# Folding two half-masked key blocks into one square per head in a windowed attention ahead of two FFNs

## Chip, cores, metric

One core of one Trainium2 chip. The metric is the device time of one execution in microseconds (us), the median of several. Work runs on TensorE (PE; its weight loads are listed as PEld), VectorE (DVE), ScalarE (ACT), GpSimd (POOL), and on DMA transfers that SyncE (SP) issues.

## The reference

Three stages in fp32, on a batch of 4, 8 heads, 576 positions and 64 values per head (2304 tokens of 512 values). The attention is causal with a window of 128 keys and a linear bias per head:

```python
rel = pos[:, None] - pos[None, :]
mask = (rel >= 0) & (rel < 128)
scores = where(mask, q @ k.T / 8 - slope[h] * abs(rel), -1e9)
attn = softmax(scores);  x = attn @ v                       # tokens x 512
h = x @ w_in;  u = h * softmax(h)                            # w_in 512 x 1024
x = ((u - mean(u)) / sqrt(var(u) + 1e-6) * g_ln) @ w_out     # w_out 1024 x 512
out = (silu(x @ w_gate) * (x @ w_val)) @ w_out2              # width 1536
```

A tile of 128 queries needs two key blocks of 128: its own block, where the keys j <= i (indices inside the block) count, and the block before, where the keys j > i count. The two masks are complements of each other. The first query tile of a batch element has only its own block.

## The kernel before

The attention runs over 20 query tiles (4 batch elements, 5 tiles t = 0 to 4; the last of each has 64 queries) and over 4 pairs of heads in each: 80 units. `score` (L329) multiplies queries by the two key blocks of two units in fp32 into one PSUM bank per unit: per head 256 columns, the block before at 0 and the own block at 128. `attend` (L368) then does, for one unit:

- L390, DVE, once per head: scores plus bias from PSUM to the tile `e` in SBUF, with the row extreme (the profile calls it CUSTOM_DVE_ANT_0, with a small accumulator read behind it);
- L395, ACT, once per head: exponential with the row sum, which is put into the same PSUM bank;
- L400 and L401, DVE: the inverse of the sums; L406 (ACT) or L408 (POOL, DVE): `e` times the inverse, both heads;
- L429, PE: each 128x128 block of `e` is turned against `ident` into a second PSUM bank, 4 turns per unit (2 where t is 0);
- L433 to L438, ACT or DVE: that bank is copied into `pt` in SBUF;
- L461, PE: values times probabilities, both blocks of keys accumulated for each head.

When the last unit of a query tile is through, its output goes to `xs` as a high and a low fp32r part (`high` L211, `low` L215), and the first FFN takes tiles of 128 tokens: `up` (L547), `flip` (L609), `down1` (L638). All its products, and those of the second FFN, are emitted by `pieces` (L539, matmuls at L543). The weights are 64-bit and are decoded on ACT, DVE and POOL (`decode`, L223): 8 blocks of `w_in` and 8 of `w_out` while the attention starts, 36 of the second FFN's later. `second_region` (L686) gives the attention's SBUF to the second FFN once the last unit is done, and starts its decoding and `gate_val` and `down` from there.

`slope` (L314) makes the scaled bias tables; `load` (L292) issues the loads of queries, keys and values through SP, and in its first call those of `base` and `ident`.

The order on every engine is made when the program is built: `Emitter` (L79) keeps the operations that could run, costs them with the formulas at L193 to L203, and gives each engine the next by earliest start and then by rank. The engines follow that order strictly; DVE operations marked `+` and POOL operations are planned as excluding each other. Eight PSUM banks (`bank_s`) are shared by all steps of this stretch; `e` has 5 buffers (EB), `pt` 3 (PTB), `v` 3, `xs` 3.

Of the kernel before, what the change touches and what calls it, by code (L numbers as in the profile page):

```python
# [17 lines left out]
B, H, S, D = 4, 8, 576, 64  # L18
NT = B * S
DM = H * D  # L20
DF1 = 1024
DF2 = 1536
P = 128
# [15 lines left out]
PXB = 2  # L39
EB = 5  # L40
PTB = 3
YS = 2
PW_2 = -0.5
LEAD = 3.2
# [136 lines left out]


@with_exitstack
def attention_then_two_ffns(ctx: ExitStack, tc: tile.TileContext, qk, v, w_in, w_out, g_ln, w2, ident_d, base_d, out):
# [22 lines left out]
    ident = const.tile([P, P], F32, name="ident")  # L207
# [82 lines left out]
    ident_ok = []  # L290

    def load(c):  # L292

        b, t = steps[c]
        n = P if t < 4 else 64
        yield raw_s
        raw[c] = [at.tile([P, 4, P], F32, tag=f"raw{x}", bufs=RAW, name=f"raw{x}") for x in range(2)]
        got = [[], []]
        for j in range(2) if c == 0 else (0,):
            part = slice(2 * j, 2 * j + 2) if c == 0 else slice(0, 4)  # L300
            for x in range(2):
                got[j].append((yield dma(raw[c][x][:, part], qk[b, t, x, :, part], 131072 if c == 0 else 262144)))
            if c == 0 and j == 0:
                chain((yield dma(base, base_d, 196608)), base_ok)
                ident_ok.append((yield dma(ident, ident_d, 65536)))
        yield v_s
        vt[c] = at.tile([P, DM], F32, tag="v", bufs=3, name="v")
        loaded[c] = yield dma(vt[c][0:n], v[b, t * P:t * P + n, :], 262144)
        for j in range(2):
            for x in got[j]:  # L310
                yield x
            prepped[c][j].settle(x.time)

    def slope(part, h):  # L314

        cs = slice(2 * P, 3 * P) if part == 0 else slice(0, 2 * P)
        n = P if part == 0 else 2 * P
# [50 lines left out]
    def attend(u):  # L368
        c, pr = divmod(u, NPAIR)
        b, t = steps[c]  # L370
        n = P if t < 4 else 64
        if t == 0:
            bs, cols, order = slice(2 * P, 3 * P), P, [1]
        elif t < 4:
            bs, cols, order = slice(P, 3 * P), 2 * P, [0, 1]
        else:
            bs, cols, order = slice(P, 2 * P + 64), P + 64, [0, 1]
        yield scored[c][pr]
        k, x = begun[u]
        sc = banks[k]  # L380
        e = at.tile([P, 2, 256], F32, tag="e", bufs=EB, name="e")
        st = at.tile([P, 8], F32, tag="st", bufs=EB, name="st")
        d = x
        for j in range(2):
            yield bias_ok[0][2 * pr + j]
            if t:
                yield bias_ok[1][2 * pr + j]
        ex, ds = [], []
        for j in range(2):
            d = yield (DVE, t_dve(cols), lambda j=j: nc.vector.tensor_tensor_reduce(  # L390
                e[0:n, j, 0:cols], sc[0:n, j * 256:j * 256 + cols], bias[0:n, 2 * pr + j, bs],
                -0.125, 3.0e38, ALU.add, ALU.min, st[0:n, j:j + 1]), [x])
            ds.append(d)
        for j, d in enumerate(ds):
            ex.append((yield (ACT, 93 + t_act(cols, True, True), lambda j=j: nc.scalar.activation(  # L395
                e[0:n, j, 0:cols], e[0:n, j, 0:cols], AF.Exp, bias=st[0:n, j:j + 1], scale=-1.0,
                accum_out=sc[0:n, j:j + 1]), [d, ds[0]])))

        def invert():
# [3 lines left out]
        def normalize(eng):  # L403
            if eng is nc.scalar:
                for j in range(2):
                    nc.scalar.activation(e[0:n, j, 0:cols], e[0:n, j, 0:cols], AF.Copy, scale=st[0:n, 6 + j:7 + j])  # L406
            else:
                eng.tensor_tensor(e[0:n, :, 0:cols], e[0:n, :, 0:cols],  # L408
                                  st[0:n, 6:8].unsqueeze(2).to_broadcast([n, 2, cols]), ALU.mult)

        x = yield (DVE, 360, invert, ex)
        em.give(bank_s, x, k)
        x = yield ([(DVEP, t_dve(2 * cols), lambda: normalize(nc.vector)),
                    (ACT, 2 * (93 + t_act(cols)), lambda: normalize(nc.scalar)),
                    (POOL, t_pool(2 * cols), lambda: normalize(nc.gpsimd))], [x])
# [6 lines left out]
        tp = banks[k].rearrange("p (k j q) -> p k j q", k=2, j=2)  # L422
# [8 lines left out]
        def store_p(copy):  # L431
            if t == 0:
                copy(pt[:, 1], tp[:, 1])  # L433
            elif t < 4:
                copy(pt, tp)  # L435
            else:
                copy(pt[:, 0, :, 0:64], tp[:, 0, :, 0:64])
                copy(pt[0:64, 1, :, 0:64], tp[0:64, 1, :, 0:64])  # L438

        x = yield (PE, 430, flip_p, ident_ok)  # L440
        em.give(e_s, x)
        w = 256 if t in (0, 4) else 512
        x = yield ([(ACT, t_act(w, False), lambda: store_p(nc.scalar.copy)),
                    (DVE, t_dve(w), lambda: store_p(nc.vector.tensor_copy))], [x])
        em.give(bank_s, x, k)
        yield x
        if pr:
            yield started[u - 1]
        else:
# [1 line left out]
            px_of[c] = yield bank_s  # L451
        px = banks[px_of[c]].rearrange("p (r q) -> p r q", r=NPAIR)

        def values():
            for kb in (1, 0):
                if kb == 0 and t == 0:
                    continue
                kp = 64 if (kb == 1 and t == 4) else P
                for j in range(2):
                    h = 2 * pr + j  # L460
                    nc.tensor.matmul(px[j * 64:(j + 1) * 64, pr, 0:n], vt[c - 1 + kb][0:kp, h * 64:(h + 1) * 64],  # L461
                                     pt[0:kp, kb, j, 0:n], start=(kb == 1), stop=(kb == 0 or t == 0),
                                     skip_group_check=True)

        x = yield (PE, 550, values, [loaded[c]])
# [6 lines left out]
            em.give(v_s, x)  # L472
        if t:
            em.give(v_s, x)
        t0 = b * S + t * P
        done = 0
        last = []
# [347 lines left out]
    nc.vector.memset(mhalf, -0.5)  # L825
    for c in range(NS):
        em.start(load(c), rank_of(c) - 0.5)
    for part in range(2):
        for h in range(H):
            em.start(slope(part, h), (-0.4, 0.15)[part] + 0.01 * h)  # L830
# [46 lines left out]
```

## Time and profile before

| | |
|---|---|
| Time, median of 3 runs | 851.47 us (851.26 to 851.69) |
| Span of the profiled execution | 850.5 us |
| PE busy | 814.5 us |
| PEld busy | 670.0 us |
| DVE busy | 424.2 us |
| ACT busy | 399.0 us |
| POOL busy | 236.1 us |

Busy time is counted per instruction and overlaps from one to the next; of a matmul it holds the whole latency, so that a PE that is "busy" all the time may still be fed slowly. The mean of one instruction therefore is not what one more of it costs: that is read from how far apart they start.

### The profile page before, as it was taken

What the parts mean: (1) busy time and instruction counts of PE and PEld (TensorE: products, weight loads), DVE (VectorE), ACT (ScalarE), POOL (GpSimd) and SP (SyncE); (2) the same over time, 40 slices, a digit from 0 to 9 for tenths busy, and PEclk for the clock granted to TensorE, in tenths of its full rate; (3) what the DMA queues carried; (4) which work ended last, traced back from release to release, by engine and by line L of the source; (5) the groups of instructions that cost most, each with busy time, mean ns of one, the idle gap of its engine ahead of it and who ended that gap; (6) DMA issues with size and microseconds to landing.
All of it is one profiled execution on the core that took longest, in us unless ns stands there. A gap on an engine that the chain in (4) does not pass through costs nothing.

```text
span 850.5 us, 13141 instructions
## 1 busy us (share of the span) xinstructions
PE 814.5 (96%) x4968; PEld 670.0 (79%) x4968; DVE 424.2 (50%) x1140; ACT 399.0 (47%) x1007; POOL 236.1 (28%) x222
## 2 busy tenths in 40 slices
PE   5699899999999999989999999999999999999997
PEld 3476678888888888889788888888888888888885
DVE  5567855554544555876511463364356336433323
ACT  7898985664755665773422531251133115211110
POOL 3566652331422222864000250052024004300000
PEclk9999999999999999999999999999999999999999
DMA  8443211221220104432400130031012002000112
GB/s 275 146 156 101 75 45 65 87 74 33 87 63 14 38 8 171 145 111 95 173 1 0 50 100 1 0 100 50 1 50 80 19 1 75 0 1 25 50 62 87
DMA packets 21839, 57.73 MB, mean 68 GB/s; under 512 B 2576, under 2 KB 3344, under 8 KB 21776
## 3 DMA queue, kind: packets, MB, share of 16 engines
q1 hardware_dynamic: 21776, 56.90, 20.3%
q8 instruction: 39, 0.64, 0.3%
q14 instruction: 24, 0.20, 0.1%
HBM read 47.45 MB, written 9.44 MB: 67 GB/s over the span
## 4 chain that ended last, share of the span: by engine, by line
PE 84%; ACT 7%; DVE 4%; DMA 3%; issue 1%; POOL 1%; SPq 0%; ACTq 0%; DVEq 0%; POOLq 0%
PE gv L543 33%; PE bank L543 21%; PE o L543 17%; PE bank L461 4%; PE bank L354 4%; PE bank L429 3%; ACT e L395 2%; PE bank L625 1%; DMA ysg<-yscr 1%; DMA dw<-w_in 1%; DVE db L243 1%; ACT e L577 1%; ACT e L406 1%; DMA raw<-qk 0%; DVE lnT L216 0%
## 5 line engine op out<-in xcount | busy, mean ns | idle before, releaser
L543 PE MATMUL gv<-y,w 128*128 128x512 f32 (+1 forms) x1392 | 314.4, 376 | 0.0
L543 PEld LDWEIGHTS gv<-y,w 128*128 128x128 f32 x1392 | 247.8, 188 | 53.8
L543 PE MATMUL o<-w,a 128*128 128x512 f32 x648 | 168.2, 394 | 1.6 <-ACT a L212 1.6
L246 POOL TENSOR_TENSOR db<-db,da 128x512 int32<-128x512 int32 x52 | 70.2, 1350 | 298.1 <-DVE db L243 289.4
L543 PEld LDWEIGHTS o<-w,a 128*128 128x128 f32 x648 | 119.9, 188 | 30.1 <-ACT a L212 2.5
L815 DVE TENSOR_TENSOR acc<-acc,o 128x512 f32<-128x512 f32 x90 | 62.0, 689 | 120.9 <-PE o L543 120.9
L543 PE MATMUL bank<-lnT,wout 128*128 128x256 f32 x864 | 118.3, 289 | 3.7 <-ACT lnT L212 2.9
L543 PEld LDWEIGHTS bank<-lnT,wout 128*128 128x128 f32 x864 | 110.1, 193 | 9.0 <-ACT lnT L212 3.1
L543 PE MATMUL bank<-win,xs 128*128 128x512 f32 x432 | 115.9, 405 | 0.2
L212 ACT CAST a<-sg 128x512 fp32r<-128x512 f32 (+1 forms) x60 | 34.7, 578 | 171.6 <-DVE sg L789 171.6
L408 POOL TENSOR_TENSOR e<-e,st 128x512 f32<-128x512 f32 (+2 forms) x60 | 55.1, 922 | 129.7 <-ACT bank L585 40.5
L543 PEld LDWEIGHTS bank<-win,xs 128*128 128x128 f32 x432 | 76.7, 189 | 17.3 <-issue 2.4
L789 DVE TENSOR_TENSOR sg<-sg,gv 128x512 f32<-128x512 f32 (+1 forms) x58 | 37.2, 641 | 105.7 <-PE gv L543 92.5
L395 ACT ACTIVATE e<-e,st 128x256 f32<-128x256 f32 (+2 forms) x160 | 74.5, 476 | 17.6 <-DVE st L390 14.4
L390 DVE CUSTOM_DVE_ANT_0 e<-bank,bias 128x256 f32<-128x256 f32 (+2 forms) x160 | 54.4, 378 | 27.0 <-PE bank L354 23.0
L787 ACT ACTIVATE sg<-gv 128x512 f32<-128x512 f32 (+1 forms) x58 | 32.4, 559 | 65.8 <-PE gv L543 60.1
L218 POOL TENSOR_TENSOR w<-db,w 128x512 fp32r<-128x512 f32 x36 | 51.9, 1443 | 27.1 <-ACT w L212 26.6
L429 PE MATMUL bank<-ident,e 128*128 128x128 f32 (+2 forms) x288 | 44.1, 281 | 11.7 <-ACT e L406 5.8
L461 PE MATMUL bank<-pt,v 128*64 128x128 f32 (+2 forms) x576 | 48.8, 283 | 5.9 <-ACT pt L435 3.1
L216 DVE TENSOR_TENSOR a<-sg,a 128x512 fp32r<-128x512 f32 (+1 forms) x60 | 42.0, 699 | 23.3 <-ACT a L212 23.3
L354 PE MATMUL bank<-raw,raw 64*128 64x128 f32 (+2 forms) x576 | 45.8, 299 | 7.6 <-DMA raw<-qk 6.5
L354 PEld LDWEIGHTS bank<-raw,raw 64*128 64x128 f32 (+1 forms) x576 | 38.0, 194 | 15.5 <-DMA raw<-qk 5.9
(61 smaller groups left out, 762.4 us busy)
## 6 DMA issues: line engine op xcount, KB each, us to landing
dw<-w SPq DMA_DIRECT2D x36, 512.0 KB, 3.6
raw<-qk SPq DMA_DIRECT2D x38, 256.0 KB, 3.8
yscr<-ys SPq DMA_DIRECT2D x9, 512.0 KB, 2.9
ysg<-yscr SPq DMA_DIRECT2D x9, 512.0 KB, 4.2
out<-acc SPq DMA_DIRECT2D x18, 256.0 KB, 2.0
dw<-w_in SPq DMA_DIRECT2D x8, 512.0 KB, 4.7
v<-v SPq DMA_DIRECT2D x16, 256.0 KB, 3.0
dw<-w_out SPq DMA_DIRECT2D x8, 512.0 KB, 3.4
```

The costliest lines, as they stand in the source:

```text
L216: ways = [(DVEP if sbuf else DVE, t_dve(n), lambda: nc.vector.tensor_sub(lo, src, hi.bitcast(F32)))]
L218: ways.append((POOL, t_pool(n), lambda: nc.gpsimd.tensor_sub(lo, src, hi.bitcast(F32))))
L246: x = yield (POOL, t_pool(512), lambda: nc.gpsimd.tensor_tensor(b.bitcast(I32), b.bitcast(I32), a.bitcast(I32), ALU.add), [x, r])
L354: nc.tensor.matmul(banks[ks[r]][0:n, o:o + w], raw[c][0][rows, 2 * qd + j, 0:n], raw[c - 1 + kb][1][rows, 2 * qd + j, 0:w], start=True, st ...
L390: d = yield (DVE, t_dve(cols), lambda j=j: nc.vector.tensor_tensor_reduce(e[0:n, j, 0:cols], sc[0:n, j * 256:j * 256 + cols], bias[0:n, 2 ...
L395: ex.append((yield (ACT, 93 + t_act(cols, True, True), lambda j=j: nc.scalar.activation(e[0:n, j, 0:cols], e[0:n, j, 0:cols], AF.Exp, bias ...
L408: eng.tensor_tensor(e[0:n, :, 0:cols], e[0:n, :, 0:cols], st[0:n, 6:8].unsqueeze(2).to_broadcast([n, 2, cols]), ALU.mult)
L429: nc.tensor.transpose(tp[0:kp, kb, j, 0:n], e[0:n, j, x * P:x * P + kp], ident[0:n, 0:n])
L461: nc.tensor.matmul(px[j * 64:(j + 1) * 64, pr, 0:n], vt[c - 1 + kb][0:kp, h * 64:(h + 1) * 64], pt[0:kp, kb, j, 0:n], start=(kb == 1), sto ...
L543: nc.tensor.matmul(o, terms[m][0], terms[m][1], start=(m == 0), stop=(m == len(terms) - 1))
L789: x = yield (DVE, t_dve(n), lambda: nc.vector.tensor_mul(sg, sg, gv[1][0]), [x, gv[1][1]])
L815: y = yield (DVE, t_dve(512), lambda o=o, tt=tt: nc.vector.tensor_add(acc[tt], acc[tt], o), [x])
```

## The change

The two halves are put into one 128x128 square per head. On the PSUM bank of the scores, a predicated copy (DVE) writes the own block's scores over those of the block before, where j <= i. Bias, exponential, normalisation and turning then work on 128 columns per head and no longer on 256. The bias table has one square for this and one for t = 0. After turning, `pt[:, 0]` is the whole square and `pt[:, 1]` a copy times the mask j <= i (DVE). The values come from `pt[:, 0]` times V of the block before plus `pt[:, 1]` times the difference of the two V tiles, `vd`, which the new task `differ` makes per query tile on POOL or DVE. The two masks `tri` are a new input, loaded behind `ident`. The number and shape of the matmuls for scores and values stay.

```diff
+VDB = 2
-    bias = at.tile([P, H, 3 * P], F32, name="bias")
-    base = at.tile([P, 3 * P], F32, name="base")
+    bias = at.tile([P, H, 2 * P], F32, name="bias")
+    base = at.tile([P, 2 * P], F32, name="base")
+    tri = at.tile([P, 2, P], F32, name="tri")
...
-                chain((yield dma(base, base_d, 196608)), base_ok)
+                chain((yield dma(base, base_d, 131072)), base_ok)
                 ident_ok.append((yield dma(ident, ident_d, 65536)))
+                tri_ok.append((yield dma(tri, tri_d, 131072)))
...
+    def differ(c):
+        n = P if steps[c][1] < 4 else 64
+        yield vd_s
+        vd[c] = at.tile([P, DM], F32, tag="vd", bufs=VDB, name="vd")
+        yield prepped[c][1]
+        x = yield ([(POOL, t_pool(DM), lambda: nc.gpsimd.tensor_sub(vd[c][0:n], vt[c][0:n], vt[c - 1][0:n])),
+                    (DVEP, t_dve(DM), lambda: nc.vector.tensor_sub(vd[c][0:n], vt[c][0:n], vt[c - 1][0:n]))],
+                   [loaded[c], loaded[c - 1]])
+        yield x
+        differed[c].settle(x.time)
...
-        e = at.tile([P, 2, 256], F32, tag="e", bufs=EB, name="e")
+        e = at.tile([P, 2, P], F32, tag="e", bufs=EB, name="e")
...
+        if t:
+            halves = sc.rearrange("p (j c) -> p j c", j=2)
+            d = yield (DVE, t_dve(2 * n), lambda: nc.vector.copy_predicated(
+                halves[0:n, :, 0:n], tri[0:n, 0, 0:n].bitcast(U32).unsqueeze(1).to_broadcast([n, 2, n]),
+                halves[0:n, :, P:P + n]), [d] + tri_ok)
...
         def flip_p():
-            for x, kb in enumerate(order):
-                kp = 64 if (kb == 1 and t == 4) else P
-                for j in range(2):
-                    nc.tensor.transpose(tp[0:kp, kb, j, 0:n], e[0:n, j, x * P:x * P + kp], ident[0:n, 0:n])
+            for j in range(2):
+                nc.tensor.transpose(tp[:, j, 0:n], e[0:n, j], ident[0:n, 0:n])
...
-        x = yield ([(ACT, t_act(w, False), lambda: store_p(nc.scalar.copy)),
-                    (DVE, t_dve(w), lambda: store_p(nc.vector.tensor_copy))], [x])
+        if t:
+            ys.append((yield (DVE, t_dve(w), lambda: nc.vector.tensor_tensor(
+                pt[0:n, 1, :, 0:n], tp[0:n, :, 0:n], tri[0:n, 1, 0:n].unsqueeze(1).to_broadcast([n, 2, n]), ALU.mult),
+                [x])))
+        ys.append((yield ([(ACT, t_act(w, False), lambda: nc.scalar.copy(pt[:, 0, :, 0:n], tp[:, :, 0:n])),
+                           (DVE, t_dve(w), lambda: nc.vector.tensor_copy(pt[:, 0, :, 0:n], tp[:, :, 0:n]))], [x])))
...
+        if t:
+            yield differed[c]
         def values():
...
+                    src = vd[c] if late else vt[c - 1] if t else vt[c]
+                    nc.tensor.matmul(px[j * 64:(j + 1) * 64, pr, 0:n], src[0:kp, h * 64:(h + 1) * 64],
+                                     pt[0:kp, late, j, 0:n], start=(late == 1 or t == 0), stop=(late == 0),
                                      skip_group_check=True)
```

## Rows read from the trace of the kernel before

**Rows 1.** The page: busy time per engine; then the chain that ended last, by engine.
```profile
PE 814.5 (96%) x4968; PEld 670.0 (79%) x4968; DVE 424.2 (50%) x1140; ACT 399.0 (47%) x1007; POOL 236.1 (28%) x222
PE 84%; ACT 7%; DVE 4%; DMA 3%; issue 1%; POOL 1%; SPq 0%; ACTq 0%; DVEq 0%; POOLq 0%
```

**Rows 2.** Busy time by stretch (us): window: length, PE, PEld, DVE, ACT, POOL, clock, DMA.
```profile
0.00:57.00 57.00, 37.22 (x306) 27.83 (x308) 32.51 (x133) 47.52 (x138) 30.23 (x30) 0.97 0.58 196
57.00:120.00 63.00, 57.05 (x415) 42.12 (x416) 47.89 (x191) 60.05 (x176) 38.08 (x39) 1.00 0.27 89
120.00:332.00 212.00, 211.23 (x1781) 177.09 (x1780) 103.14 (x444) 129.82 (x404) 58.62 (x73) 1.00 0.16 53
332.00:400.00 68.00, 63.82 (x450) 59.76 (x449) 53.87 (x91) 40.00 (x81) 40.65 (x33) 0.97 0.41 134
```

**Rows 3.** Chain that ended last, in order of time: start, length (us), what.
```profile
188.60 1.31 PE bank L429 x12
...
231.97 0.61 PE bank L429 x8
```

**Rows 4.** Turns of PE by form, three stretches: 0 to 57, to 120, to 340.
```profile
L429 PE MATMUL bank<-ident,e 128*128 128x128 f32 x52 | 11.1, 348 | 10.0 <-ACT e L406 5.6 <-POOL e L408 4.4
...
L429 PE MATMUL bank<-ident,e 128*128 128x128 f32 x40 | 7.1, 289 | 1.8 <-POOL e L408 1.4 <-ACT e L406 0.2 <-DVE lnT L216 0.2
...
L429 PE MATMUL bank<-ident,e 128*128 128x128 f32 x132 | 20.1, 279 | 0.0
L429 PE MATMUL bank<-ident,e 64*128 64x64 f32 x24 | 3.6, 239 | 0.0
```

**Rows 5.** ACT by form, 0 to 57: count, busy us, mean ns, idle before.
```profile
L395 ACT ACTIVATE e<-e,st 128x256 f32<-128x256 f32 x24 | 11.9, 508 | 1.0 <-DVE st L390 0.8
L435 ACT COPY pt<-bank 128x512 f32<-128x512 f32 x11 | 6.5, 594 | 2.7 <-PE bank L429 2.6
L406 ACT ACTIVATE e<-e,st 128x256 f32<-128x256 f32 x10 | 4.4, 503 | 0.0
L395 ACT ACTIVATE e<-e,st 128x128 f32<-128x128 f32 x8 | 3.1, 405 | 0.4 <-DVE st L390 0.3
L319 ACT ACTIVATE bias<-base 128x256 f32<-128x256 f32 x8 | 2.9, 410 | 0.0
L433 ACT COPY pt<-bank 128x256 f32<-128x256 f32 x4 | 1.3, 374 | 0.0
```

**Rows 6.** The same view, 57 to 120, the exponential with the most instructions.
```profile
L395 ACT ACTIVATE e<-e,st 128x256 f32<-128x256 f32 x19 | 9.5, 509 | 0.2
```

**Rows 7.** DVE by form, 57 to 120.
```profile
L390 DVE CUSTOM_DVE_ANT_0 e<-bank,bias 128x256 f32<-128x256 f32 x20 | 7.5, 420 | 0.7 <-PE bank L354 0.7
L216 DVE TENSOR_TENSOR xs<-bank,xs 128x256 fp32r<-128x256 f32 x5 | 1.9, 419 | 0.4 <-ACT xs L212 0.4
L390 DVE CUSTOM_DVE_ANT_0 e<-bank,bias 128x128 f32<-128x128 f32 x8 | 1.9, 284 | 0.0
L216 DVE TENSOR_TENSOR xs<-bank,xs 128x512 fp32r<-128x512 f32 x1 | 0.7, 683 | 0.0
```

**Rows 8.** Timeline of DVE, then of ACT, near 47 us: start, length (us), instruction.
```profile
46.81 0.42 DVE L390 CUSTOM_DVE_ANT_0 e<-bank,bias 128x256 f32<-128x256 f32 x1 [1.83 <-PE bank L354]
47.16 0.42 DVE L390 CUSTOM_DVE_ANT_0 e<-bank,bias 128x256 f32<-128x256 f32 x1
...
47.69 0.51 ACT L395 ACTIVATE e<-e,st 128x256 f32<-128x256 f32 x1 [0.84 <-DVE st L390]
```

**Rows 9.** ACT by form, 120 to 340, the copies of the turned bank.
```profile
L435 ACT COPY pt<-bank 128x512 f32<-128x512 f32 x30 | 17.3, 600 | 14.2 <-PE bank L429 14.1
```

**Rows 10.** POOL by form, first 120 us: the subtractions for the first weights.
```profile
L218 POOL TENSOR_TENSOR win<-db,win 128x512 fp32r<-128x512 f32 x8 | 10.4, 1302 | 7.0 <-ACT win L212 6.9
```

**Rows 11.** Timeline of SP (an issue), then of PE, in the first 8 us.
```profile
2.56 0.43 SPq L203 DMA_DIRECT2D ident<-ident  x1
...
7.74 1.23 PE L354 MATMUL bank<-raw,raw 64*128 64x128 f32 x8 [0.92 <-DMA raw<-qk]
```

More of the change, by code (lines that the diff above doesn't have):

```diff
@@ L183, in attention_then_two_ffns @@
 @with_exitstack
-def attention_then_two_ffns(ctx: ExitStack, tc: tile.TileContext, qk, v, w_in, w_out, g_ln, w2, ident_d, base_d, out):
+def attention_then_two_ffns(ctx: ExitStack, tc: tile.TileContext, qk, v, w_in, w_out, g_ln, w2, ident_d, base_d, tri_d, out):
     nc = tc.nc
@@ L289, in attention_then_two_ffns @@
     prepped = [[Done(), Done()] for _ in range(NS)]
-    ident_ok = []
+    ident_ok, tri_ok = [], []
+    vd, vd_s = {}, Slots(VDB)
+    differed = {c: Done() for c in range(NS)}
     def load(c):
@@ L314, in slope @@
     def slope(part, h):
-        cs = slice(2 * P, 3 * P) if part == 0 else slice(0, 2 * P)
-        n = P if part == 0 else 2 * P
+        cs = slice(P, 2 * P) if part == 0 else slice(0, P)
+        n = P
         yield base_ok
@@ L371, in attend @@
         n = P if t < 4 else 64
[L372 to L377, printed above, removed]
+        bs, late = (slice(0, P), 1) if t else (slice(P, 2 * P), 0)
         yield scored[c][pr]
@@ L384, in attend @@
         for j in range(2):
[L385 to L388, printed above, removed]
+            yield bias_ok[late][2 * pr + j]
+        if t:
[3 more added lines that the diff above has]
+                halves[0:n, :, P:P + n]), [d] + tri_ok)
+        ex, ds, x = [], [], d
         for j in range(2):
-            d = yield (DVE, t_dve(cols), lambda j=j: nc.vector.tensor_tensor_reduce(
-                e[0:n, j, 0:cols], sc[0:n, j * 256:j * 256 + cols], bias[0:n, 2 * pr + j, bs],
+            d = yield (DVE, t_dve(P), lambda j=j: nc.vector.tensor_tensor_reduce(
+                e[0:n, j], sc[0:n, j * 256:j * 256 + P], bias[0:n, 2 * pr + j, bs],
                 -0.125, 3.0e38, ALU.add, ALU.min, st[0:n, j:j + 1]), [x])
@@ L394, in attend @@
         for j, d in enumerate(ds):
-            ex.append((yield (ACT, 93 + t_act(cols, True, True), lambda j=j: nc.scalar.activation(
-                e[0:n, j, 0:cols], e[0:n, j, 0:cols], AF.Exp, bias=st[0:n, j:j + 1], scale=-1.0,
+            ex.append((yield (ACT, 93 + t_act(P, True, True), lambda j=j: nc.scalar.activation(
+                e[0:n, j], e[0:n, j], AF.Exp, bias=st[0:n, j:j + 1], scale=-1.0,
                 accum_out=sc[0:n, j:j + 1]), [d, ds[0]])))
@@ L421, in attend @@
         turned[u].settle(0.0)
-        tp = banks[k].rearrange("p (k j q) -> p k j q", k=2, j=2)
+        tp = banks[k][:, 0:2 * P].rearrange("p (j q) -> p j q", j=2)
         pt = at.tile([P, 2, 2, P], F32, tag="pt", bufs=PTB, name="pt")
         def flip_p():
-            for x, kb in enumerate(order):
-                kp = 64 if (kb == 1 and t == 4) else P
-                for j in range(2):
-                    nc.tensor.transpose(tp[0:kp, kb, j, 0:n], e[0:n, j, x * P:x * P + kp], ident[0:n, 0:n])
[L431 to L440, printed above, removed]
-        em.give(e_s, x)
-        w = 256 if t in (0, 4) else 512
-        x = yield ([(ACT, t_act(w, False), lambda: store_p(nc.scalar.copy)),
-                    (DVE, t_dve(w), lambda: store_p(nc.vector.tensor_copy))], [x])
-        em.give(bank_s, x, k)
-        yield x
+            for j in range(2):
+                nc.tensor.transpose(tp[:, j, 0:n], e[0:n, j], ident[0:n, 0:n])
+        x = yield (PE, 218, flip_p, ident_ok)
+        em.give(e_s, x)
+        w = 2 * n
+        ys = []
+        if t:
[4 more added lines that the diff above has]
+                           (DVE, t_dve(w), lambda: nc.vector.tensor_copy(pt[:, 0, :, 0:n], tp[:, :, 0:n]))], [x])))
+        for y in ys:
+            yield y
+        em.give(bank_s, max(ys, key=lambda y: y.time), k)
         if pr:
@@ L452, in attend @@
         px = banks[px_of[c]].rearrange("p (r q) -> p r q", r=NPAIR)
+        if t:
+            yield differed[c]
         def values():
[L455 to L458, printed above, removed]
+            for late in (1, 0) if t else (0,):
+                kp = n if late else P
                 for j in range(2):
                     h = 2 * pr + j
-                    nc.tensor.matmul(px[j * 64:(j + 1) * 64, pr, 0:n], vt[c - 1 + kb][0:kp, h * 64:(h + 1) * 64],
-                                     pt[0:kp, kb, j, 0:n], start=(kb == 1), stop=(kb == 0 or t == 0),
+                    src = vd[c] if late else vt[c - 1] if t else vt[c]
+                    nc.tensor.matmul(px[j * 64:(j + 1) * 64, pr, 0:n], src[0:kp, h * 64:(h + 1) * 64],
+                                     pt[0:kp, late, j, 0:n], start=(late == 1 or t == 0), stop=(late == 0),
                                      skip_group_check=True)
@@ L474, in attend @@
             em.give(v_s, x)
+            em.give(vd_s, x)
         t0 = b * S + t * P
@@ L827, in attention_then_two_ffns @@
         em.start(load(c), rank_of(c) - 0.5)
+    for c in range(NS):
+        if steps[c][1]:
+            em.start(differ(c), rank_of(c) - 0.3)
     for part in range(2):
@@ L863 @@
     g = np.ascontiguousarray(f["moe_g_ln"].reshape(KF1, P).T)
-    i, c = np.arange(P)[:, None], np.arange(3 * P)[None, :]
-    rel = np.where(c < P, i - c, 2 * P + i - c)
-    base = np.where((rel >= 0) & (rel < P), -8.0 * rel, -8.0e9 * 2 ** H).astype(np.float32)
+    i, c = np.arange(P)[:, None], np.arange(P)[None, :]
+    rel = i - c
+    base = np.concatenate([np.where(rel >= 0, -8.0 * rel, -8.0 * (P + rel)),
+                           np.where(rel >= 0, -8.0 * rel, -8.0e9 * 2 ** H)], axis=1).astype(np.float32)
+    tri = np.stack([rel >= 0, rel <= 0], axis=1).astype(np.float32)
     ident = np.eye(P, dtype=np.float32)
     arrays = {"qk": qk, "v": v, "w_in": wide["moe_w_in"], "w_out": wide["moe_w_out"], "g_ln": g,
-              "w2": np.ascontiguousarray(w2), "ident": ident, "base": base}
+              "w2": np.ascontiguousarray(w2), "ident": ident, "base": base, "tri": tri}
     nc = bacc.Bacc("TRN2", target_bir_lowering=False, num_devices=1)
```

11 lines of the change are left out of this document (5 added, 6 removed).

## Prediction

> **What bounds the kernel now.** I read the page first: PE is busy 96% of the span, DVE 50%, ACT 47%, and PE holds 84% of the chain that ended last [rows 1]. That is an average over unlike stages, so the next view is the busy time by stretch [rows 2]. From 120 to 332 us PE is busy 211.2 of 212 us, while ACT has 129.8 and DVE 103.1: here the PE's own work sets the time, and what other engines gain is worth nothing. From 57 to 120 us PE is busy 57.0 of 63, but ACT is busy 60.0 of 63: two engines are near their end. In the first 57 us PE has 37.2 us and ACT 47.5: ACT, which decodes weights beside the attention, leads the chain there. After 332 us no attention is left. So the change must be costed three times: as PE work, as ACT work in the first 120 us, and as DVE work everywhere.
>
> The price of one turn is not its mean (279 ns) but its distance from the next: 12 in a row took 1.31 us of the chain, 109 ns each; of the 64-query form 8 took 0.61 us, 76 ns each [rows 3].
>
> **PE, removed.** Units with t > 0 go from 4 turns to 2. From 120 us on there are 132 turns of 128 columns and 24 + 24 of the two 64-query forms (the second form's row, not shown, has the count of the first) [rows 4]; the 8 units there with t = 0 keep their 16. Saved: (132 - 16) / 2 = 58 x 0.109 = 6.3 us, and 48 / 2 = 24 x 0.076 = 1.8 us; **8.1 us**, all on the path. From 57 to 120 us: (40 - 8) / 2 = 16, 1.7 us and a little for the 64-query forms, worth something only if ACT and DVE follow. Before 57 us (52 - 8) / 2 = 22 turns, 2.4 us, beside a PE that waits in any case. Scores and values keep their matmuls, at no cost or gain.
>
> The Trainium skill ("TensorE: Matmul & The Clock Gate", Part 4: PE-mode transpose) gives about 275 ns for one turn inside a kernel, which is also the trace's mean of 279 ns [rows 4]. By it the 128 turns that go would be an estimated 35 us and the time some 816 us; the start distances of [rows 3] say that this is a latency, and they decide.
>
> **ACT, removed.** Prices in the first 57 us [rows 5]: an exponential 508 to 405 ns, 24 of them, 2.5 us; a copy of the turned bank 594 to 374, 11, 2.4 us; a normalisation of 503 and a line of the second bias table of 410, which lose the same 128 columns, by as much as the exponential each, 10 and 8, 1.8 us. With 0.1 for two 64-row exponentials: **6.8 us** of 47.5. From 57 to 120 us, by the same prices, 19 exponentials [rows 6] 2.1, 7 copies 1.7, 4 copies in two parts that become one 1.0, 8 normalisations 0.8, 64-row exponentials 0.4: **6.0 us** of 60.0.
>
> **DVE, added.** The product with the mask reads PSUM and writes SBUF, 256 columns: the nearest row is the subtraction of that shape, 419 ns [rows 7]. The predicated copy is in no row. Lower end: 284 ns, the row of half the columns; upper end: 683 ns, the row of twice the columns, if mask and data go one after the other; I take 419, the row of its own size and of two operands. Two bias steps go from 420 to 284. A unit: 0.42 + 0.42 - 2 x 0.136 = **+0.57 us** (+0.83 at the upper end, +0.43 at the lower); a 64-query unit about +0.45. That is 7.7 us in the first 57 us (12 units and 2 of 64 queries), 6.6 us from 57 to 120 (10 and 2), 20 us later. DVE then has 40 of 57, 54.5 of 63 and 123 of 212 us: room, but from 57 to 120 us it replaces ACT as the fullest engine. There ACT and DVE together go from 107.9 to 108.5 us: the load is moved, not taken away.
>
> **A new wait.** The product (DVE) and the copy (ACT) read the same PSUM bank. The trace shows that such pairs are kept apart: at 47.69 us the first head's exponential, which writes into the scores' bank, starts only when the second head's bias step on that bank, begun at 47.16, is done; the first had begun at 46.81, and ACT had idled 0.84 us [rows 8]. So whichever of product and copy comes second waits for the first, 0.37 to 0.42 us, and with it all that is queued behind it on its engine: on ACT the next exponentials and weight decoding, on DVE the maxima of the first FFN. The plan that fixes the order knows nothing of it. Price on ACT at most 12 x 0.42 = 5.0 us in the first 57 us and the same from 57 to 120; below nothing it can't be, a wait never shortens anything. I take all of it, by that row. Net of ACT: -6.8 + 5.0 = **-1.8 us**, and -6.0 + 5.0 = **-1.0 us**, where PE can follow with its 1.7 us. Ends: -6.8 and -6.0 if the waits fall into idle time; +2.7 and +2.2 if the predicated copy is also at its upper end (0.42 + 0.26 = 0.68 us for 14 units less 6.8, for 12 less 6.0). From 120 us on both engines have idle time that hides it; without that cover it is 38 units x 0.42.
>
> The Trainium skill ("PSUM — Partial Sum Buffer", PSUM bank collisions raise a hardware error) says that two engines must not use one bank and quadrant at once, two reads included. The trace agrees, by the wait in [rows 8]; without the rule the sum would be 10 us lower, at the low case below.
>
> **Small things.** The load of `tri` is one more issue on SP (0.43 us, as `ident`) ahead of the second half of the first queries and keys, of the first values and of the next weight block; PE waits 0.92 us for that half today [rows 11]: **+0.4 us** (0 to 0.9). `differ` adds 16 subtractions of about 1.3 us on POOL [rows 10], whose normalisations get half as wide; POOL is busy about half of the first 120 us [rows 2], so nothing, but it would wait there for a V tile to land, with weight decoding queued behind it: up to 1 us at the start. From 332 to 400 us I take no change; PE idles 4.2 us there, so 4 us either way is the bound.
>
> **Sum.** 850.5 - 8.1 - 1.8 - 1.0 + 0.4 = 840.0 us of span; the median of the runs is 1.0 us above the profiled span, so **841.0 us**.
>
> **Rivals.**
> *The start follows ACT.* The bank waits fall into idle time and the first 120 us shrink by ACT's 12.8 us: 851.5 - 8.1 - 12.8 + 0.4 = 831.0. For it: ACT leads there [rows 2]. Against: DVE's load grows by as much.
> *DVE stands still behind PE; slower than before.* The product waits for the turn, and PE may be in a run of six FFN products. The ACT copies, which do that now, idle 14.2 us for it in 30 instructions, 0.47 us each [rows 9]. On DVE the same wait stops the maxima and subtractions that feed PE. Where more than 0.28 us of it per unit reaches PE (38 units after 120 us, against 8.1 + 2.8 - 0.4 = 10.5 us of gain), all is lost; at 0.37 to 0.47 the time is 855 to 859. Against it: DVE is idle half of that stretch and `up` has three tiles in flight.
> *Given back at the change of stage.* PE comes to 332 us earlier, but the second FFN's decoding on DVE and POOL doesn't move up with it; up to 8.1 us is lost between 332 and 400 us: 849.1. Against: it starts when the last unit is done, which is earlier too.
>
> **How the numbers follow.** Forecast (836 to 847) 0.60; start follows ACT 0.15; given back 0.10, half of it within 0.2%; DVE stands still 0.13; 0.02 for a start that loses what PE gains, within 0.2%. 0.2% is 1.7 us, about what a measurement of this kernel can tell from no change. Faster 0.60 + 0.15 + 0.05 = 0.80; same 0.05 + 0.02 = 0.07; slower 0.13. The range runs from the low case, 831, to the upper ends of the start with the PE gain, 851.5 - 8.1 + 2.7 + 2.2 + 0.9 + 4 = 853; the case of a slower kernel is left out.
>
> **What would show it.** Right: 160 turns, still near 109 ns apart; the last attention matmul some 11 us earlier; ACT below 56 of 63 us in the stretch that ended at 120 us; copies and products one after the other, one of them with DVE or ACT as its releaser; PE idle below 2 us between start and last unit. Wrong: a predicated copy much over 0.42 us; PE waits on `pt` of DVE, or on maxima, in the steady stretch; the distance from the last attention matmul to the second FFN's steady run grown by several us.

## The result, and the profile after

The changed kernel takes **843.91 us** (843.08 to 845.34) against 851.58 us for the kernel before in the same session: ratio 0.9911, 95% interval 0.9897 to 0.9925, a gain of 7.7 us. The forecast was 841.0 us, in a range of 831 to 853. The sign, the mechanism on TensorE and the range were right; 2.9 us of the expected gain did not come.

The profiled execution of after has a span of 843.5 us; that execution took 845.3 us, the longest of the four. Its page, the engines' busy time and the chain that ended last, against [rows 1]:

```profile
PE 804.2 (95%) x4840; PEld 659.1 (78%) x4840; DVE 440.8 (52%) x1268; ACT 374.8 (44%) x995; POOL 236.2 (28%) x236
PE 80%; DVE 7%; ACT 6%; POOL 3%; DMA 2%; issue 1%; SPq 0%; POOLq 0%; ACTq 0%; DVEq 0%
```

128 fewer instructions on PE, 24 us less of ACT, 17 us more of DVE. DVE's share of the chain has risen from 4% to 7%, PE's has fallen from 84% to 80%. The same stretches as in [rows 2] (window: length, PE, PEld, DVE, ACT, POOL, granted clock, DMA):

```profile
0.00:57.00 57.00, 37.72 (x322) 26.73 (x322) 38.47 (x179) 44.69 (x154) 31.75 (x36) 0.91 0.63 207
57.00:120.00 63.00, 55.87 (x369) 42.81 (x370) 49.17 (x190) 53.04 (x157) 38.82 (x39) 0.89 0.25 81
120.00:332.00 212.00, 211.32 (x1732) 175.84 (x1731) 125.02 (x544) 120.63 (x406) 57.75 (x82) 1.00 0.19 63
332.00:400.00 68.00, 61.98 (x433) 56.91 (x432) 44.54 (x77) 38.48 (x73) 39.40 (x32) 1.00 0.37 123
```

From 120 to 332 us PE is busy 211.3 of 212 us, as it was, so turns taken out there are time taken out. Ahead of 120 us ACT is relieved about as forecast: exponentials, copies, normalisations and bias tables together take 12.4 us less there (12.8 forecast), though ACT's busy time as a whole falls by 9.9. DVE is loaded about as forecast: product and predicated copy take 19.2 us, the bias steps 6.4 less, 12.8 more in all (14.3 forecast), though its busy time, in which instructions overlap, rises by 7.2. PE is busy no less: 93.6 us in these two stretches against 94.3. The granted clock has fallen, from 0.97 and 1.00 to 0.91 and 0.89. At the costs of a start to the next start in a row (turn 109 ns, product with `w_in` 233, product with `w_out` 115, matmul of scores or values about 70), PE gets an estimated 72.1 us of work done in the first 120 us, against 76.5 before; the 44 turns that went there are 4.5 us, so it is the same work less its removed turns, in the same time. **By this estimate the start gained nothing.**

The new instructions, on VectorE in the first 57 us (count, busy us, mean ns, idle before and its releaser), and a pair of turns in the chain (start, length):

```profile
L405 DVE CUSTOM_DVE_ANT_0 e<-bank,bias 128x128 f32<-128x128 f32 x34 | 8.7, 283 | 1.7 <-PE bank L371 1.3
L448 DVE TENSOR_TENSOR pt<-bank,tri 128x256 f32<-128x256 f32 x12 | 5.0, 420 | 1.8 <-ACT pt L451 1.0 <-PE bank L441 0.8
L400 DVE COPY_PREDICATED bank<-tri,bank 128x256 f32<-128x256 uint32 x12 | 4.8, 422 | 2.7 <-PE bank L371 2.7
L400 DVE COPY_PREDICATED bank<-tri,bank 64x128 f32<-64x128 uint32 x4 | 1.0, 278 | 0.0
```

```profile
122.60 0.22 PE bank L441 x2
```

The copy of the turned square on ACT, first in the first 57 us, then from 120 to 340 us:

```profile
L451 ACT COPY pt<-bank 128x256 f32<-128x256 f32 x16 | 5.9, 375 | 4.9 <-DVE pt L448 3.1 <-PE bank L441 1.7
```

```profile
L451 ACT COPY pt<-bank 128x256 f32<-128x256 f32 x35 | 12.3, 382 | 21.4 <-DVE pt L448 16.9 <-PE bank L441 4.0
```

Where [rows 9] had copies waiting for turns, they now wait for the product on their bank: 16.9 of 21.4 us in the steady stretch, where it costs nothing, and 3.1 us in the first 57. PE's own longest waits over the whole run (total, times, longest):

```profile
PE bank L371 <- DMA raw<-qk: 6.3, 2, 5.6
PE bank L441 <- ACT e L421: 5.4, 3, 3.3
PE bank L555 <- ACT lnT L213: 4.2, 2, 2.7
PE bank L637 <- DVE lnT L217: 3.4, 1, 3.4
PE bank L441 <- POOL e L423: 2.8, 5, 1.7
PE bank L472 <- DVE pt L448: 2.7, 5, 0.7
PE bank L472 <- ACT pt L451: 2.7, 3, 1.8
```

The order of the start has moved too, since the plan that interleaves attention and weight decoding has new prices. POOL's last low part for `w_in`, before and then after, and the stretch around it, 55 to 60 and 60 to 65 us, before and then after:

```profile
56.03 1.27 POOL L218 TENSOR_TENSOR win<-db,win 128x512 fp32r<-128x512 f32 x1
```

```profile
62.46 1.47 POOL L219 TENSOR_TENSOR win<-db,win 128x512 fp32r<-128x512 f32 x1 [1.32 <-ACT win L213]
```

```profile
55.00:60.00 5.00, 4.82 (x53) 3.50 (x51) 2.06 (x15) 4.90 (x17) 3.73 (x4) 1.00 0.68 239
60.00:65.00 5.00, 5.00 (x37) 3.60 (x35) 3.69 (x11) 4.90 (x18) 1.69 (x3) 1.00 0.24 76
```

```profile
55.00:60.00 5.00, 4.25 (x36) 3.48 (x36) 3.75 (x20) 3.53 (x16) 1.47 (x3) 0.50 0.02 6
60.00:65.00 5.00, 4.72 (x35) 3.64 (x32) 2.29 (x13) 4.06 (x16) 3.68 (x4) 0.50 0.81 253
```

`w_in` is ready 6.6 us later, attention runs further ahead of it, and PE works these ten microseconds at a granted clock of 0.50, the lower of its two levels, 1.2 of 2.4 GHz. Ahead of the drop, from 40 to 55 us, it was busy 10.9 of 15 us.

### The profile page after: what moved, and what is told of

It is laid out like the page before. It is cut to its first block, busy times and chain, and to the rows that moved or that the text cites. A ratio compares the mean times of both kernels' runs of the same rounds, so it can differ in the third digit from the quotient of the medians.

```text
span 843.5 us, 12981 instructions
## 1 busy us (share of the span) xinstructions
PE 804.2 (95%) x4840; PEld 659.1 (78%) x4840; DVE 440.8 (52%) x1268; ACT 374.8 (44%) x995; POOL 236.2 (28%) x236
## 4 chain that ended last, share of the span: by engine, by line
PE 80%; DVE 7%; ACT 6%; POOL 3%; DMA 2%; issue 1%; SPq 0%; POOLq 0%; ACTq 0%; DVEq 0%
PE gv L555 34%; PE bank L555 18%; PE o L555 18%; PE bank L472 4%; PE bank L371 4%; PE bank L441 2%; POOL db L247 2%; PE bank L637 1%; DVE db L244 1%; DMA ysg<-yscr 1%; ACT e L410 1%; DVE db L241 1%; DVE e L591 1%; DMA dw<-w_in 1%; ACT da L236 1%
## 5 line engine op out<-in xcount | busy, mean ns | idle before, releaser
L410 ACT ACTIVATE e<-e,st 128x128 f32<-128x128 f32 (+1 forms) x160 | 63.0, 401 | 21.1 <-DVE st L405 19.0
L213 ACT CAST w<-db 128x512 fp32r<-128x512 f32 x35 | 21.7, 620 | 64.3 <-POOL db L247 64.2
L423 POOL TENSOR_TENSOR e<-e,st 128x256 f32<-128x256 f32 (+1 forms) x58 | 35.1, 612 | 44.0 <-DVE st L416 37.0
L405 DVE CUSTOM_DVE_ANT_0 e<-bank,bias 128x128 f32<-128x128 f32 (+1 forms) x160 | 40.4, 282 | 9.2 <-PE bank L371 4.5
L451 ACT COPY pt<-bank 128x256 f32<-128x256 f32 (+1 forms) x79 | 26.4, 357 | 38.6 <-DVE pt L448 27.3
```

The source lines that it names most:

```text
L213: return [(ACT, t_act(n, sbuf), lambda: nc.scalar.copy(hi, src)), (DVEP if sbuf else DVE, t_dve(n, sbuf), lambda: nc.vector.tensor_copy(hi ...
L405: d = yield (DVE, t_dve(P), lambda j=j: nc.vector.tensor_tensor_reduce(e[0:n, j], sc[0:n, j * 256:j * 256 + P], bias[0:n, 2 * pr + j, bs], ...
L410: ex.append((yield (ACT, 93 + t_act(P, True, True), lambda j=j: nc.scalar.activation(e[0:n, j], e[0:n, j], AF.Exp, bias=st[0:n, j:j + 1], ...
L423: eng.tensor_tensor(e[0:n], e[0:n], st[0:n, 6:8].unsqueeze(2).to_broadcast([n, 2, P]), ALU.mult)
```

## The experiments

All times are medians; the interval is that of the ratio to the kernel before, times 851.5 us. "Clock" is the mean granted clock of the first 120 us of the one execution that was profiled.

| kernel | us | against before (interval) | clock |
|---|---|---|---|
| before | 851.5 | | 0.99 |
| **after** | **843.9** | -7.6 (-8.8 to -6.4) | 0.90 |
| turns_twice | 852.3 | +1.2 (+0.3 to +2.2) | 0.93 |
| no_product | 841.2 | -10.3 (-11.8 to -8.7) | 0.94 |
| no_predicated | 844.6 | -7.2 (-8.9 to -5.4) | 0.90 |
| no_differ | 844.8 | -6.6 (-7.9 to -5.4) | 0.91 |
| win_first | 844.1 | -7.7 (-9.0 to -6.2) | 0.90 |
| held_back | 846.5 | -5.1 (-6.3 to -3.8) | 0.90 |
| decode_three | 843.4 | -7.5 (-9.0 to -6.0) | 0.91 |
| product_from_copy | 852.2 | +0.8 (-0.2 to +1.6) | 0.87 |
| copy_on_dve | 850.9 | -0.4 (-1.3 to +0.5) | 0.85 |
| product_from_e | 848.6 | -2.9 (-3.9 to -1.9) | 0.89 |
| before_short_exp | 849.3 | -1.8 (-2.7 to -0.8) | 0.97 |
| before_reordered | 850.4 | -0.9 (-1.8 to -0.1) | 0.96 |

Of the kernels that do all the work none is faster than after by more than the intervals; decode_three equals it.

**Undo the PE part alone.**

```diff
+        tq = banks[k][:, 2 * P:4 * P].rearrange("p (j q) -> p j q", j=2)
...
+            if t:
+                for j in range(2):
+                    nc.tensor.transpose(tq[:, j, 0:n], e[0:n, j], ident[0:n, 0:n])
```


> Undoes the PE part alone: in the changed kernel, every unit with t > 0 turns its two squares twice, the second time into the unused half of the same bank, where nobody reads it; the planned order of all engines stays as it is. 128 more turns. If a turn costs what the chain of before says (109 and 76 ns), the stretch in which PE is busy throughout gets 58 x 0.109 + 24 x 0.076 = 8.1 us longer and the whole at most 12.9 us: 852 to 857 us. Rival, the turns are hidden and the gain came from ACT and DVE: 844 to 846 us. A third possibility lies between: turns in the first 120 us fall into PE's idle time, so 852 and not 857.

852.34 us, 8.4 us above after (about 7 to 10 by the two intervals). The removed turns are 12.9 us by their start distances (96 x 0.109 + 32 x 0.076); those from 120 us on are the prediction's 8.1. So the turns of the steady stretch are worth what they take, the 4.8 us of turns ahead of it are worth little or nothing (under 2), and all the rest of the change together costs 1.2 us (0.3 to 2.2), where the prediction had it gain 2.4.

**Each addition alone taken out, the order kept** (so the mask of the own block is missing once in the values and once in the scores, and then the difference of V).

```diff
-            ys.append((yield (DVE, t_dve(w), lambda: nc.vector.tensor_tensor(
...
+            ys.append((yield (DVE, t_dve(w), lambda: None, [x])))
...
-                                     pt[0:kp, late, j, 0:n], start=(late == 1 or t == 0), stop=(late == 0),
+                                     pt[0:kp, 0, j, 0:n], start=(late == 1 or t == 0), stop=(late == 0),
```


> The changed kernel without the product with the mask on DVE (its second half of the values reads the plain copy instead, so the own block's probabilities are not masked); the planned order stays, the product's place in it is empty. Theory 'bank': the ACT copy waits for the product, 5.2 us of ACT in the first 120 us, and that makes the first FFN's weights late: without it they come some 4 us earlier and the time is 839 to 841 us. Theory 'load': DVE has 10 us less to do in the first 120 us, the same 839 to 841 us. Theory 'order': the weights are late because their DVE steps are queued behind DVE steps that wait for scores and turns, whatever the product costs: the last block of w_in still comes after 62 us, 842 to 844 us.

841.16 us: the product, with every wait that hangs on it, costs 2.7 us (about 1 to 5 by the two intervals). The last block of `w_in` was done at 59.3 us instead of 63.9.

```diff
-            d = yield (DVE, t_dve(2 * n), lambda: nc.vector.copy_predicated(
...
+            d = yield (DVE, t_dve(2 * n), lambda: None, [d] + tri_ok)
```


> The changed kernel without the predicated copy (the scores of the own block are left out, the square holds the block before alone); the planned order stays. Theory 'load': DVE has about 10 us less to do in the first 120 us, 839 to 841 us. Theory 'bank': nothing changes there, 843 to 845 us. Theory 'order': the bias step now waits for the scores in the place of the predicated copy, so the weights stay late, 842 to 844 us.

844.64 us, the same as after, though VectorE is busy 80.3 us in the first 120 instead of 87.6. VectorE's load as such is therefore probably not what the start pays for: about as much taken out in the product's place counts, in the predicated copy's place it does not. (With four executions each, the intervals of the two runs still touch.)

```diff
-        x = yield ([(POOL, t_pool(DM), lambda: nc.gpsimd.tensor_sub(vd[c][0:n], vt[c][0:n], vt[c - 1][0:n])),
...
+        x = yield ([(POOL, t_pool(DM), lambda: None), (DVEP, t_dve(DM), lambda: None)],
...
-                    src = vd[c] if late else vt[c - 1] if t else vt[c]
+                    src = vt[c] if late else vt[c - 1] if t else vt[c]
```


> The changed kernel without the 16 subtractions of V, all other work in the same order; the masked copies multiply V itself, so the output lacks that difference. Theory 'differences hidden': 843.2 to 844.5, no change from the 843.9 with them, since GpSimd is busy 28% of the span. Theory 'differences in the way' (GpSimd is in the decode's chain, and a subtraction that waits for V's transfer holds up the decode and the normalisations queued behind it): the last block of w_in ends 1 to 4 us earlier than 63.9 and the time is 841 to 842.5.

844.81 us: the differences are hidden, as forecast. (`w_in` was ready at 61.5 us instead of 63.9, and that too bought nothing.)

**Is it the late `w_in`?** Three runs with the same instructions in another order.

```diff
-PW_IN = [-0.6, -0.3, -0.29, -0.28, 0.07, 0.08, 0.09, 0.1]
+PW_IN = [-0.6, -0.3, -0.29, -0.28, -0.27, -0.26, -0.25, -0.24]
```


> The changed kernel with the second half of w_in ranked ahead of all attention units (the ranks 0.07 to 0.10 of its four blocks become -0.27 to -0.24); only the order changes, no work. Theory 'order': the last block of w_in is done by about 58 us (63.9 in the changed kernel, 57.3 in the one before), FFN products fill PE earlier, the granted clock no longer falls between 54 and 68 us, and some 4 us of the 4.7 us lost from 57 to 120 us come back: 839 to 841 us. Theories 'load' and 'bank': the engines have the same work, 843 to 845 us.

844.11 us; `w_in` at 64.0 us, hardly any instruction changed place. This edit did not do what it was for, and so tells nothing but that ranks do not decide there.

```diff
+HOLD = {2: 3, 3: 5, 4: 6, 5: 7}
+        if c in HOLD:
+            yield win_ok[HOLD[c] // 4][HOLD[c] % 4]
         yield prepped[c][qd]
```


> The changed kernel with the scores of query tiles 2 to 5 ordered behind blocks 4, 6, 7 and 8 of w_in (tiles counted from 0); it computes the same. Theory 'late w_in' (what the start was to give went because attention, now cheaper, runs ahead of the decode of w_in, so the first FFN comes 6.6 us later, TensorE has only short attention matmuls from 40 to 65 us and its granted clock stands at the lower level from 54 to 68 us): the last block of w_in ends at 55 to 60 us instead of 63.9, the clock between 54 and 68 us is back above 0.9, and the time is 839.5 to 842. Theory 'waits' (what went is the copies' waiting for the masked product on their bank; when w_in ends decides nothing): 843 to 845.5. Holding attention back may itself cost: then over 845.5.

846.45 us. `w_in` was ready at 54.9 us, earlier than in the kernel before, the granted clock from 55 to 105 us was 1.00, and the time rose by 2.5 us: the clock stood at the lower level from 25 to 35 and from 45 to 50 us instead (in after, besides 55 to 65, from 25 to 30), and its mean over the first 120 us was the same 0.90.

```diff
+    da1_s, db1_s = Slots(3), Slots(3)
...
-        a = dec.tile([P, 512], U32, tag="da", bufs=2, name="da")
+        a = pool.tile([P, 512], U32, tag="da", bufs=nb, name="da")
...
-        b = dec.tile([P, 512], U32, tag="db", bufs=2, name="db")
+        b = pool.tile([P, 512], U32, tag="db", bufs=nb, name="db")
...
+                                      pool=at, da_s=da1_s, db_s=db1_s, nb=3)
```


> The changed kernel with three blocks of w_in in decode at a time instead of two, in buffers of their own; it computes the same, and attention is ordered as the decode leaves room. Theory 'late w_in': the last block ends at 55 to 60 us instead of 63.9, the stretch from 57 to 120 us loses 2 to 4 us less, the time is 839.5 to 842. Theory 'waits': 843 to 845. If both buffers are no limit and the decode only follows its engines' queues, w_in stays at 62 to 65 us and the time at 843 to 845.

843.41 us, no difference from after; `w_in` at 56.2 us, the clock at 1.00 from 50 to 70 us and at 0.50 from 25 to 35. The theory of the late `w_in` falls by this run: the edit did what it should, and the time stayed. held_back agrees, but says less, since over 845.5 us its expectation had it that holding attention back costs by itself. As a control, another order of the kernel before:

```diff
-PW_IN = [-0.6, -0.3, -0.29, -0.28, 0.07, 0.08, 0.09, 0.1]
+PW_IN = [-0.6, -0.3, -0.29, -0.28, 1.2, 1.3, 1.4, 1.5]
```


> The kernel before with the ranks of the last four blocks of w_in at 1.2 to 1.5 instead of 0.07 to 0.1, a control: no instruction is added, removed or made shorter, only the planned order of the first 120 us changes. Theory 'order counts' (what the start gives or costs hangs on the order in which the planner interleaves attention and decode, by a few us either way): 2 us or more off the 851.5 in either direction. Theory 'order is indifferent, instructions count': 850.5 to 852.5.

850.40 us, 0.9 us below (0.1 to 1.8). It moved less than the 2 us that the theory "order counts" asked for, and its interval ends just beside no change. Taken with held_back, an order alone is worth from about -1 to +2.5 us here.

**Is it the wait on the bank?** Three ways of taking away what the copy waits for.

```diff
+        y = yield ([(ACT, t_act(w, False), lambda: nc.scalar.copy(pt[:, 0, :, 0:n], tp[:, :, 0:n])),
...
+        em.give(bank_s, y, k)
...
+                eng.tensor_tensor(pt[0:n, 1, :, 0:n], pt[0:n, 0, :, 0:n],
+                                  tri[0:n, 1, 0:n].unsqueeze(1).to_broadcast([n, 2, n]), ALU.mult)
...
+            ys.append((yield ([(DVEP, t_dve(w), lambda: product(nc.vector))], [y])))
```


> The changed kernel with the masked product taken from the SBUF copy of the turned square, after that copy, on VectorE as before, so that product and copy share no PSUM bank; it computes the same. Theory 'bank wait' (the 2.7 us that go away without the product are the copy's waiting on the product's bank): ScalarE's copies idle no more for the product (6 us of 21 in the first 120 us before), time 841 to 842.5. Theory 'product's own time' (they are VectorE's 0.42 us a pair and the values' later start): the product now starts 0.4 us later behind the copy, time 844 to 846.

852.15 us, 8.2 us above after and worse than either theory had it. No copy waits for a product any more, but a product now waits for its copy, and in the first 120 us the product of 128x256, which now reads two SBUF tiles, takes 681 ns instead of 419. VectorE's idle time behind the copies (11.9 us) all lies after 120 us, where PE is busy throughout. What is lost is PE's: the values wait 10.9 us for the product, nearly all of it in the first 120 us, against 2.7 in after, and these 8.2 us more are as much as the run lost. PE's wait on `pt` (in total, times, longest):

```profile
PE bank L475 <- DVE pt L453: 10.9, 8, 2.8
```

```diff
-        ys.append((yield ([(ACT, t_act(w, False), lambda: nc.scalar.copy(pt[:, 0, :, 0:n], tp[:, :, 0:n])),
+        ys.append((yield ([(ACT, t_act(w, False), lambda: (nc.vector.tensor_copy if t else nc.scalar.copy)(pt[:, 0, :, 0:n], tp[:, :, 0:n])),
```


> The changed kernel, its instructions in their order, with the copy of the turned square in query tiles 1 to 4 of a batch on VectorE, right behind the masked product there, instead of on ScalarE; it computes the same. No copy on ScalarE waits for a product any more, ScalarE is some 10 us less busy in the first 120 us and VectorE as much more. Theory 'bank wait' (without the product the time fell 2.7 us because the copies no longer stood in ScalarE's queue behind it): 840 to 842.5. Theory 'product's own time on the path or VectorE's load': 845 to 849.

850.94 us. The wait of ScalarE is gone, ScalarE is 7 us less busy in the first 120 us and VectorE 4 us more, and the time rises by 7.0 us, above both theories. The first 120 us of copy_on_dve, then of after:

```profile
0.00:120.00 120.00, 92.14 (x640) 68.04 (x640) 91.94 (x375) 90.70 (x282) 70.32 (x75) 0.85 0.42 140
```

```profile
0.00:120.00 120.00, 93.59 (x691) 69.54 (x692) 87.64 (x368) 97.73 (x311) 70.57 (x75) 0.90 0.43 141
```

PE has 640 matmuls in these 120 us instead of 691. Its waits for VectorE's `pt` are 4.1 us in the whole run against 2.7, so they alone do not account for this loss.

```diff
-                pt[0:n, 1, :, 0:n], tp[0:n, :, 0:n], tri[0:n, 1, 0:n].unsqueeze(1).to_broadcast([n, 2, n]), ALU.mult),
+                pt[0:n, 1, :, 0:n], e[0:n, :, 0:n], tri[0:n, 1, 0:n].unsqueeze(1).to_broadcast([n, 2, n]), ALU.mult),
```


> The changed kernel, its instructions in their order, with the masked product taken from the square before its turn, in SBUF, instead of from the turned square in the PSUM bank; the late values use an unturned square, so the output is not attention's. VectorE has a product as before (some 0.05 us longer, by the 476 ns of one between SBUF tiles against 418), but it shares no bank with the copy, and ScalarE's copies wait for the turns alone. Theory 'bank wait' (what the product costs, 2.7 us, is the copies' waiting): 841 to 842.5, as without any product. Theory 'VectorE's time' (it is the 0.4 us a pair in VectorE's queue): 843 to 845.5, as with the product on the bank.

848.55 us, 4.6 us above after; both theories missed. The row says why; product and copy in the first 120 us, and one product beside GpSimd:

```profile
L448 DVE TENSOR_TENSOR pt<-e,tri 128x256 f32<-128x256 f32 x18 | 14.1, 786 | 0.0
L451 ACT COPY pt<-bank 128x256 f32<-128x256 f32 x26 | 9.5, 378 | 6.4 <-PE bank L441 6.4
```

```profile
31.47 1.49 DVE L448 TENSOR_TENSOR pt<-e,tri 128x256 f32<-128x256 f32 x1
31.29 1.38 POOL L247 TENSOR_TENSOR db<-db,da 128x512 int32<-128x512 int32 x1 [2.98 <-DVE db L244]
```

ScalarE's copies wait for turns alone, so the bank wait is gone; but the product, read from SBUF, takes 786 ns instead of 419: of the 22 products in these 120 us, 12 take over 600 ns, each of them begun while a GpSimd instruction ran and ended only after it. The 22 products, the 64-query ones included, take 16.0 us, where 24 took 9.5 in after: 0.34 us more each, 7.4 in all. A run meant to take the wait away at equal VectorE time has put 7.4 us on VectorE in the product's place, and the time rose by 4.6. With no_product (9.5 us out of that place, 2.7 us gained) it points to VectorE's time there being paid for, at 0.3 to 0.6 of itself. It does not prove it: no_product takes the waits away too, and in product_from_e GpSimd is 2.0 us busier in these 120 us. That the waiting on the bank costs anything on its own no run shows.

**What is ScalarE's relief worth?**

```diff
-                e[0:n, j, 0:cols], e[0:n, j, 0:cols], AF.Exp, bias=st[0:n, j:j + 1], scale=-1.0,
+                e[0:n, j, 0:P], e[0:n, j, 0:P], AF.Exp, bias=st[0:n, j:j + 1], scale=-1.0,
```


> The kernel before, its instructions in their order, with each attention exponential over the first 128 of its columns instead of 256 (in the 64-query tile of 192); what is left out is half of the exponentials, so the weights are not softmax weights. It takes from ScalarE the part of the relief that the prediction counted in exponentials, some 0.2 us in each of about 50 in the first 120 us, 10 us in all, and adds no wait. Theory 'the start follows ScalarE': 841.5 to 846. Theory 'the start's pace is set by the order across engines and the hand-overs, ScalarE's free time goes into idle': 849.5 to 851.5, and the first 120 us of the profile hold as much TensorE work as before within 1 us.

849.31 us, 1.8 us gained (0.8 to 2.7): between the theories. The expectation's 10 us was a slip. The exponential goes from 509 to 401 ns, 43 of them in the first 120 us, which with the short ones makes 5.0 us. ScalarE's relief at the start is thus worth some 0.36 us for each us taken off (0.16 to 0.54), not 1.

## Why the prediction was right, and where it missed

- **PE, -8.1 us: right.** 160 turns are left, a pair still takes 0.22 us in the chain, PE is busy 211.3 of 212 us in the steady stretch, and putting the 128 turns back costs 8.4 us. The start distances of [rows 3] were the price. One term is a little large: the 64-query turns that went are those of 64x64, and these start 56 ns apart, not 76, so the 24 of them are 1.3 us and the whole 7.7. The Trainium skill ("TensorE: Matmul & The Clock Gate", Part 4: PE-mode transpose) has about 275 ns for a turn; the trace agrees with that as a duration (283 ns in the mean from 120 to 332 us), and the 816 us estimated from it are 28 us off.
- **Prices on VectorE and ScalarE: right.** The predicated copy takes 422 ns (419 was taken, from ends of 284 and 683), the product 420, the bias step 283, the exponential 400, the copy 375.
- **The start, -1.8 - 1.0 us: wrong; this is the step that failed.** It took ScalarE's 12.8 us of relief at full value, set against it a wait on the bank at its upper bound, 10.0 us, and put the added 14.3 us on VectorE at nothing ("room"). The runs show another account. The relief is worth about 0.36 of itself: an estimate of 12.8 x 0.36 = 4.6 us (2.0 to 6.9). The copies' wait on the product is 5 us, not 10, in the first 120. The product with its waits costs 2.7 us, the predicated copy nothing that could be measured. That would still be -1.9 us; measured is +1.2 (0.3 to 2.2) for everything but the turns, `tri` included. Some 3 us stay **unexplained** (an estimate; the runs' intervals allow anything from none to 6). The order of the start, which the change shifts as well, moves the time by -1 to +2.5 us on its own; the rest may lie there or in the clock (the next point), but no run shows it. That the forecast of the start came within 4 us of the measured is luck in part: a relief taken 8 us too high stood against a wait taken 5 us too high.
- **The granted clock was in no term.** Its mean in the first 120 us fell from 0.99 to 0.90; between the levels 0.5 and 1.0 that is some 24 us at the lower one, against 3 before. Six products with `w_in` in after (start, length), at the lower level and then at the higher:

```profile
65.54 2.59 PE L555 MATMUL bank<-win,xs 128*128 128x512 f32 x6
71.73 1.66 PE L555 MATMUL bank<-win,xs 128*128 128x512 f32 x6
```

  They start 427 ns apart there instead of 233. From such distances the lower level took an estimated 11 us of PE's time in the start, at most, against 2 before; part of it PE would have waited in any case. That is more than the 3 us without an explanation, so the clock may be all of them. Over the ten kernels with 160 turns the time goes with it: 841.2 us at 0.94, 843.4 to 844.8 at 0.90 to 0.91, 848.6 at 0.89, 850.9 and 852.2 at 0.85 and 0.87; held_back (846.5 at 0.90) stands apart. Executions of one and the same program differ in that way too: copy_on_dve took 848.8 us with a clock of 0.986 over the whole span and 851.9 with 0.975. Whether the waits bring the clock down or the clock makes PE late, these runs do not say. Among the kernels with the 288 turns it does not hold: before_short_exp is faster than before at 0.97 against 0.99.
- **From span to median, +1.0 us: not a cost.** It came from which execution had been profiled; each execution's time is some 1.8 us above its own span (845.3 and 843.5 in after).
- **`tri` and the differences: right.** The issue of `tri` takes 0.43 us on SP, PE waits 0.70 us for the second half of the first load (0.92 before), and no_differ gains nothing.
- **The rivals.** *The start follows ACT* needed a relief at full value and falls with before_short_exp. *DVE stands still behind PE* did not come in the steady stretch: PE waits 2.7 us in all for the product. But its mechanism exists at the start: in product_from_copy, where the product comes later and takes longer, PE waits 10.9 us for it and the whole gain is lost. *Given back at the change of stage*: in part. The last attention matmuls on PE's timeline (start, length), before and then after:

```profile
331.80 0.49 PE L461 MATMUL bank<-pt,v 64*64 64x64 f32 x6
```

```profile
327.49 0.34 PE L472 MATMUL bank<-pt,v 128*64 128x64 f32 x4
```

The attention ends 4.5 us earlier (327.8 against 332.3), not the 11 that the prediction named: attention and first FFN share the stretch in another proportion, so this milestone was badly chosen. The steady run of `o`, further down PE's timeline, begins at 406.77 us instead of 413.88; these 7.1 us are the whole difference of the two spans (7.0), so nothing is lost behind it. Between 332 and 425 us PE's time without work, by start distances, is an estimated 8.8 us against 7.1: 1.7 us went there, within the 4 us either way that the prediction left.

## What to carry to other kernels

Where one engine is busy 99% of a stretch, work taken off it is time, at the distance from start to start in a row and not at the mean duration; where two or three engines hand pairs of heads on to one another, work taken off the fullest of them is worth less than itself (here, in one run, about a third), and what is put on another one seems to count by its place in the pair's chain, not by that engine's busy share. A planner's order is part of such a change: forecast a start stage with some 2 us either way for the order alone, and read its granted clock. Ahead of a masked product, look where it reads: the same product from PSUM was untouched by GpSimd, and from SBUF it nearly doubled (786 ns against 419).

## What the runs showed of the hardware

- A VectorE product of two SBUF tiles, 128x256, takes 417 ns in the mean in product_from_e where no GpSimd instruction overlaps it (19 of them) and 715 ns where one does (29), up to 1.49 us; from PSUM and SBUF, in after, it is 419 and 418 ns. The Trainium skill ("SBUF — State Buffer", SBUF: two separate sides) says that an instruction of VectorE with two SBUF inputs and one of GpSimd that reads SBUF use a shared pair of ports, which the first to start holds for its whole length while the other waits; the timeline above agrees, a product begun 0.18 us behind a GpSimd instruction of 1.38 us took 1.49.
- A predicated copy of 128x256 from PSUM to the same bank, its mask in SBUF, takes 422 ns, no more than a product of that shape; with 64x128, 278 ns.
- The granted clock of a PE that is not idle can stand at the lower level: 0.50 from 55 to 65 us of after, with PE busy 9.0 of these 10 us and 10.9 of the 15 us ahead of them. A view of busy time alone does not show it: in the first 120 us PE's busy time was the same 94 us before and after.
